# A decode step of attention and ReGLU on one core: the dummy products at the end taken out, and the first 26 rows of wo loaded and multiplied in two pieces

## The chip, the cores and the metric

The kernel runs on one core of a Trainium2 chip. The metric is the device time of one execution in microseconds. Beside it stands a profile of one execution: its span goes from the first to the last instruction, and its times are counted from the span's start.

## What is computed

Four sequences take one decode step. With x of shape (4, 1, 512):

```python
g = sigmoid((x * gate_w).sum(-1, keepdims=True))
q = (x @ wq) as 32 heads of 128
k, v = last 4096 rows of the caches of 8 heads, each shared by 4 heads of q
o = softmax(q k^T / sqrt(128)) v
a = o.reshape(4, 1, 4096) @ wo                 # wo: 4096 x 512
gate, up = x @ W_gate, x @ W_up                # 512 x 1792
b = (gate * (gate > 0) * up) @ W_down          # W_down: 1792 x 512
return g * a + (1 - g) * b
```

All inputs are bf16. K and V of the window are 32 MiB each, and the weights some 13 MiB together, so that the kernel reads 81 MB and computes little with it.

## The kernel before

**Staging.** Work on the caches goes in 8 sets (a sequence and half of its key heads), 4 MiB of K and 4 MiB of V each, in two buffers of each kind (`Ksb`, `Vsb`). All large loads are issued by SP in one order: wq, K and V by turns, W_gate and W_up into the buffer of K of set 6, the last V, W_down into the buffer of V of set 6, and then wo into `Wbig`, where wq was. SP waits with a load until PE has done with the buffer. The issue of W_down waits for the values of set 6, and the loads of wo stand behind it in SP's program.

**A set.** PE transposes K (line 366, f32 words that hold two bf16 each), ACT and DVE copy the result back (lines 371 and 373), PE forms the scores (line 387), DVE and ACT make the softmax's numerators (lines 395 to 431), PE multiplies them with V (line 442), and `combine` (lines 456 to 466) sums and scales into `oq`, already times g. PE's program for the sets from 2 on is a loop of three turns (`Fori`), and what follows the loop is written out.

**The end, which the change touches.** After the last set's scores PE runs, in this order: `combine` of set 6, `gateup` (line 472), the last set's `values` (line 442), its `combine`, and then the output products, which all sum into one bank of PSUM, `AB`:

- 56 products of `hT` with W_down (14 rows of 128-wide tiles, 4 column blocks `cb` each);
- the products of `oq` with wo. Each partition holds 32 rows of wo (`Wo3[:, i, :]`, i from 0 to 31), and each row gives 4 products of 128 columns, one for each column block.

Every product goes through `product` (line 543). The four column blocks sit in four 32-column strips of PE's array (`tile_position=(0, 32 * cb)`) and write to four strips of 32 partitions of the bank.

**The cuts of wo.** `WO_CUTS` names the rows at which the load of wo is cut: `(0, 26, 30)` makes a load of rows 0 to 25 (3328 KB, event `("WO", 0)`), one of rows 26 to 29 (512 KB, `("WO", 1)`), both at line 248, and then two of the last two rows, each of half the columns (128 KB each, `("WOL", u)`, line 251). The products of a piece wait for its load. The last 8 products end in two events `("ACC", u)`, for which DVE (line 568) and ACT (line 570) wait, each casting two blocks of 128 columns into `outr`. SP waits for the four casts and stores `outr` (line 594).

**The dummies.** `warm(n)` (line 548) issues n products of a 128x128 identity with 256 columns of `mask` into the bank `SCB[1]`, which nobody reads. Four stand ahead of each piece of wo that is cut by `WO_CUTS`, and four ahead of the last two rows: 12 in all.

**Waits.** `emit_list` gives an instruction a wait only where the engine hasn't already waited for that semaphore's value; every load of wo has a semaphore of its own.

Of the kernel before, what the change touches and what calls it, by code (L numbers as in the profile page):

```python
# [19 lines left out]
NSET = 8  # L20
# [8 lines left out]
NPIECE = 2  # L29
NBANK = 4  # L30
NFILL = 16
WO_CUTS = (0, 26, 30)
ACT_TAKES = (0, 1, 4, 6, 8, 9, 11, 13, 14)
LOOP_FIRST = 2
LOOP_TURNS = 3
# [107 lines left out]
def bass_gated_mix__sliding_block_cached__glu_gated_reglu__decode_kernel(  # L143
# [13 lines left out]
    with ExitStack() as ctx:  # L157
        def sb(name, shape, dt):
            return ctx.enter_context(nc.sbuf_tensor(name, shape, dt))
# [7 lines left out]
        mask = sb("mask", [128, 512], BF16)  # L167
        ident = sb("ident", [128, 128], BF16)
# [33 lines left out]
        SCB = banks[NTR:NTR + NSC]  # L202
# [10 lines left out]
        P = Program()  # L213
# [31 lines left out]
        wo_src = A_wo.rearrange("(p i) w -> p (i w)", p=128)  # L245
        for k in range(len(WO_CUTS) - 1):
            lo, hi = 512 * WO_CUTS[k], 512 * WO_CUTS[k + 1]
            P.dma("sp", lambda e, lo=lo, hi=hi: e.dma_start(Wbig[:, lo:hi], wo_src[:, lo:hi]), ("WO", k), [("Q",)])
        wo_src3 = A_wo.rearrange("(p i) w -> p i w", p=128)
        for u in range(2):  # L250
            P.dma("sp", lambda e, u=u: e.dma_start(Wo3[:, WO_CUTS[-1]:32, 256 * u:256 * u + 256],
                                                   wo_src3[:, WO_CUTS[-1]:32, 256 * u:256 * u + 256]), ("WOL", u), [("Q",)])

# [50 lines left out]
        for t in range(4):  # L304
            P.op("pe", lambda e, t=t: e.matmul(FB[:, 32:36], gwB[:, t * 128:(t + 1) * 128], xT[:, t, 0:4],
                                               start=(t == 0), stop=(t == 3)),
# [5 lines left out]
        for half in range(2):  # L312
            for t in range(4):
                for g in range(4):
# [3 lines left out]
                        start=(t == 0), stop=(t == 3), tile_position=(0, 32 * g)),  # L318
# [223 lines left out]
        def product(stat, mov, cb, start, stop, name, waits):  # L542
            P.op("pe", lambda e: e.matmul(AB[32 * cb:32 * cb + 4, 0:128], stat, mov[:, 128 * cb:128 * cb + 128],  # L543
                                          start=start, stop=stop, tile_position=(0, 32 * cb)), name, waits)

        def warm(n):
            for k in range(n):
                P.op("pe", lambda e: e.matmul(SCB[1][:, 0:256], ident[:, :], mask[:, 0:256], start=True, stop=True),  # L548
                     None, [("MASK",), ("SCC", NSET - 1, NBANK - 1), ("SCC", NSET - 1, 1)])

        for i in range(NFT):
            for cb in range(4):
                product(hT[:, 4 * i:4 * i + 4], Wd[:, i, :], cb, i == 0, False, None,
                        [("WD",), ("H",), ("SCC", NSET - 1, NBANK - 1)])
        for k in range(len(WO_CUTS) - 1):
            warm(4)
            for i in range(WO_CUTS[k], WO_CUTS[k + 1]):
                for cb in range(4):
                    product(oq3[:, :, i], Wo3[:, i, :], cb, False, False, None, [("WO", k), ("OQ", NSET - 1)])
        warm(4)  # L560
        for u in range(2):
            for i in range(WO_CUTS[-1], 32):
                for cb in (2 * u, 2 * u + 1):
# [76 lines left out]
```

## Time and profile before

| what | before |
|---|---|
| median of 3 runs | 199.1 us (198.62 to 200.11) |
| the profiled execution's own time | 199.63 us |
| its span | 198.4 us |
| mean granted TensorE clock | 0.871 |
| busy: PE, DVE, ACT, POOL | 138.5, 105.3, 63.8, 7.3 us |
| read from HBM | 81.01 MB, 408 GB/s over the span |

How to read it: the page cuts the span into 40 slices of 4.96 us and gives a digit for each, the busy share in tenths. PEclk is the share of TensorE's clock that was granted, 1.00 being full. In a list in order of time, a row has start, duration, engine, line, operation, the tile written and those read, and the shape; the bracket at the end is the idle time ahead of it and what ended that. PE's matmuls are pipelined: a group of n products that lasts t has not n times the mean duration of one, since they overlap, and the end of the group is the end of the last. The chain of waits is followed back from the last instruction, at each step to what released it.

### The profile page before, as it was taken

Reading aid. Unit: us, or ns where it says so; the run is one execution under the profiler, and the core shown is the slowest. Engines: PE = TensorE matmul, PEld = TensorE weight load, DVE = VectorE, ACT = ScalarE, POOL = GpSimd, SP = SyncE. Lnnn points to the kernel's source line nnn. Section 1 sums busy time; section 2 is a strip of 40 time slices with the busy share of each in tenths; the row PEclk is TensorE's granted clock in tenths of the full one; section 3 lists DMA queues with packets and bytes.
Section 4 is the critical chain, followed back from the end, with each engine's and each line's share of the span. In section 5 each row is a group of like instructions: output and inputs, shape, how many; then the busy total and the mean of one; then the engine's idle time right before and its main releaser. Section 6 shows DMA issues by size and latency. Waiting matters only on the chain.

```text
span 198.4 us, 3970 instructions
## 1 busy us (share of the span) xinstructions
PE 138.5 (70%) x1708; PEld 105.3 (53%) x1708; DVE 105.3 (53%) x282; ACT 63.8 (32%) x112; POOL 7.3 (4%) x37
## 2 busy tenths in 40 slices
PE   0135399689399939973997499759946996708446
PEld 0112387556288638743874487458626864206343
DVE  1204046895568557952785278529760986740101
ACT  2002135663074307511651165127503650400001
POOL 7300000000000000000000000000000000000000
PEclk9999999999759988995799669979995899666957
DMA  6999999999999999999999999999999999999950
GB/s 225 456 449 436 436 423 426 423 423 415 436 443 453 423 426 424 429 439 429 423 423 423 436 456 424 429 423 429 443 436 429 409 406 461 423 419 458 398 199 4
DMA packets 3741, 81.17 MB, mean 409 GB/s; under 512 B 393, under 2 KB 914, under 8 KB 1042
## 3 DMA queue, kind: packets, MB, share of 16 engines
q1 hardware_dynamic: 3720, 81.01, 95.6%
q8 instruction: 8, 0.13, 0.3%
q14 instruction: 3, 0.02, 0.0%
q10 hardware_dynamic: 10, 0.01, 0.0%
HBM read 81.01 MB, written 0.00 MB: 408 GB/s over the span
## 4 chain that ended last, share of the span: by engine, by line
DMA 58%; PE 34%; DVE 5%; issue 1%; SPq 0%; ACT 0%; DVEq 0%
DMA Ksb<-in_A_k_cache_dram 46%; PE bank L366 21%; DMA Wbig<-in_A_wo_dram 12%; PE bank L387 5%; DVE Ksb L373 3%; PE bank L442 2%; PE bank L543 2%; PE bank L456 2%; PE bank L548 1%; DVE sc L395 1%; DVE pT L431 1%; DVE mq L402 0%; ACT Ksb L371 0%; DVE negmax L416 0%; SPq L588 0%
## 5 line engine op out<-in xcount | busy, mean ns | idle before, releaser
L366 PE MATMUL bank<-identw,Ksb 128*128 128x128 f32 x512 | 79.4, 318 | 26.5 <-DMA Ksb<-in_A_k_cache_dram 26.5
L366 PEld LDWEIGHTS bank<-identw,Ksb 128*128 128x128 f32 x512 | 70.0, 166 | 36.1 <-DMA Ksb<-in_A_k_cache_dram 28.3
L371 ACT COPY Ksb<-bank 128x512 f32<-128x512 f32 x72 | 41.2, 586 | 87.6 <-PE bank L366 87.5
L373 DVE COPY Ksb<-bank 128x512 f32<-128x512 f32 x56 | 37.6, 685 | 43.7 <-PE bank L366 43.5
L395 DVE CUSTOM_DVE_ANT_0 sc<-bank,mask 128x512 bf16<-128x512 f32 x32 | 21.8, 680 | 7.5 <-PE bank L387 7.3
L442 PE MATMUL bank<-Vsb,pT 128*32 128x256 bf16 x512 | 20.7, 291 | 6.7 <-DMA Vsb<-in_A_v_cache_dram 6.7
L387 PE MATMUL bank<-Ksb,qS 128*32 128x512 bf16 x256 | 20.2, 391 | 4.3 <-DVE Ksb L373 4.1
L442 PEld LDWEIGHTS bank<-Vsb,pT 128*32 128x32 bf16 x512 | 13.4, 101 | 13.5 <-issue 9.8
L431 DVE STREAM_TRANSPOSE pT<-sc 128x1024 bf16<-128x1024 bf16 x16 | 19.7, 1236 | 1.4 <-ACT sc L424 1.3
L424 ACT ACTIVATE sc<-sc,negmax 128x1024 bf16<-128x1024 bf16 x16 | 18.4, 1150 | 5.3 <-DVE negmax L416 5.2
L456 PEld LDWEIGHTS bank<-osb,Wsel 128*64 128x64 f32 x128 | 8.2, 139 | 5.5 <-issue 2.9
L456 PE MATMUL bank<-osb,Wsel 128*64 128x32 f32 x128 | 9.1, 225 | 2.0 <-DVE osb L448 2.0
L387 PEld LDWEIGHTS bank<-Ksb,qS 128*32 128x32 bf16 x256 | 4.2, 95 | 11.5 <-DVE Ksb L373 6.5
L570 ACT CAST outr<-bank 4x128 bf16<-4x128 f32 x2 | 0.5, 258 | 25.0 <-PE bank L543 25.0
L543 PE MATMUL bank<-Wbig,oq 128*4 128x128 bf16 x128 | 3.8, 303 | 5.1 <-DMA Wbig<-in_A_wo_dram 5.1
L448 DVE COPY osb<-bank 128x256 f32<-128x256 f32 x8 | 3.4, 420 | 6.7 <-PE bank L442 6.7
L568 DVE CAST outr<-bank 4x128 bf16<-4x128 f32 x2 | 0.6, 282 | 11.6 <-PE bank L543 11.6
L298 PE MATMUL bank<-identw,xw 5*128 5x5 f32 x4 | 0.6, 264 | 8.5 <-DVE xw L292 8.5
L543 PEld LDWEIGHTS bank<-Wbig,oq 128*4 128x4 bf16 x128 | 3.1, 120 | 6.0 <-DMA Wbig<-in_A_wo_dram 5.4
L348 POOL COPY qS<-qW 128x64 bf16<-128x64 bf16 x8 | 1.8, 236 | 119.1 <-PE bank L387 106.6
L316 PE MATMUL bank<-Wbig,xT 128*32 128x512 bf16 x32 | 3.6, 631 | 3.0 <-DMA Wbig<-in_A_wq_dram 3.0
L416 DVE TENSOR_SCALAR negmax<-mall 32x1 f32<-32x1 f32 x32 | 4.6, 144 | 1.0
(60 smaller groups left out, 55.2 us busy)
## 6 DMA issues: line engine op xcount, KB each, us to landing
Ksb<-in_A_k_cache_dram SPq DMA_DIRECT2D x8, 4096.0 KB, 23.1
Vsb<-in_A_v_cache_dram SPq DMA_DIRECT2D x8, 4096.0 KB, 32.2
Wbig<-in_A_wq_dram SPq DMA_DIRECT2D x1, 4096.0 KB, 12.4
Wbig<-in_A_wo_dram SPq DMA_DIRECT2D x1, 3328.0 KB, 24.3
Ksb<-in_B_W_gate_dram SPq DMA_DIRECT2D x1, 1792.0 KB, 18.8
Ksb<-in_B_W_up_dram SPq DMA_DIRECT2D x1, 1792.0 KB, 22.7
Vsb<-in_B_W_down_dram SPq DMA_DIRECT2D x1, 1792.0 KB, 16.7
Wbig<-in_A_wo_dram SPq DMA_DIRECT2D x1, 512.0 KB, 25.1
```

Source lines behind the costliest of these rows:

```text
L316: P.op("pe", lambda e, half=half, t=t, g=g, col=col: e.matmul(SCB[half][32 * g:32 * g + 32, 0:512], xT[:, t, :], Wq3[:, t, col:col + 512], ...
L366: P.op("pe", lambda e, bk=bk, cc=cc, c=c, s=s: e.transpose(bk[:, cc * 128:(cc + 1) * 128], Kw[:, s % 2, c * 128:(c + 1) * 128], identw[:, :]),
L371: P.op("act", lambda e: e.copy(dst, bk[:, :]), ("KTC", s, i), [("KT", s, i)], sem="va")
L373: P.op("dve", lambda e: e.tensor_copy(dst, bk[:, :]), ("KTC", s, i), [("KT", s, i)], sem="vd")
L387: P.op("pe", lambda e, a=a, o=o: e.matmul(bk[32 * a:32 * a + 32, 0:512], qS[:, s % 2, o, :], k4[:, 16 * bank:16 * bank + 16, 32 * a:32 * a ...
L395: P.op("dve", lambda e: e.tensor_tensor_reduce(sc[:, s % 2, bank * 512:(bank + 1) * 512], bk[:, :], mask[:, :], 1.0, LOWEST, ALU.add, ALU.max,
L416: P.op("dve", lambda e, a=a: e.tensor_scalar(negmax[32 * a:32 * a + 32, par:par + 1], mall[:, 0:1], -SCALE, None, op0=ALU.mult), ("NEGMAX" ...
L424: P.op("act", lambda e: e.activation(sc[:, par, k * PW:(k + 1) * PW], sc[:, par, k * PW:(k + 1) * PW], ACTF.Exp, bias=negmax[:, par:par + ...
L431: P.op("dve", lambda e: e.transpose(pT[:, par, k * PW:(k + 1) * PW], sc[:, par, k * PW:(k + 1) * PW]), ("PTT", s, k), [("EXP", s, k), ("PV ...
L442: P.op("pe", lambda e, c=c, g=g, blk=blk: e.matmul(OB[32 * g:32 * g + 32, 0:256], pT[:, par, 32 * blk:32 * blk + 32], Vsb[:, par, 256 * bl ...
L456: P.op("pe", lambda e, k=k, lo=lo: e.matmul(FB[r, 384:416], Wsel[:, lo:lo + 64], osb[:, par, 32 * k:32 * k + 32], start=(k == 0), stop=(k ...
L543: P.op("pe", lambda e: e.matmul(AB[32 * cb:32 * cb + 4, 0:128], stat, mov[:, 128 * cb:128 * cb + 128], start=start, stop=stop, tile_positi ...
```

## The change

`WO_CUTS` gets one more cut, so that rows 0 to 25 come as a load of rows 0 to 15 (2048 KB) and one of rows 16 to 25 (1280 KB), each with a semaphore and a wait of its own; the products of rows 0 to 15 wait for the first alone. The order of the products is the same. `warm` and its three places are taken out. wo now comes in five loads.

```diff
-WO_CUTS = (0, 26, 30)
+WO_CUTS = (0, 16, 26, 30)
...
-        def warm(n):
-            for k in range(n):
-                P.op("pe", lambda e: e.matmul(SCB[1][:, 0:256], ident[:, :], mask[:, 0:256], start=True, stop=True),
-                     None, [("MASK",), ("SCC", NSET - 1, NBANK - 1), ("SCC", NSET - 1, 1)])
-
         for i in range(NFT):
             for cb in range(4):
                 product(hT[:, 4 * i:4 * i + 4], Wd[:, i, :], cb, i == 0, False, None,
                         [("WD",), ("H",), ("SCC", NSET - 1, NBANK - 1)])
         for k in range(len(WO_CUTS) - 1):
-            warm(4)
             for i in range(WO_CUTS[k], WO_CUTS[k + 1]):
                 for cb in range(4):
                     product(oq3[:, :, i], Wo3[:, i, :], cb, False, False, None, [("WO", k), ("OQ", NSET - 1)])
-        warm(4)
         for u in range(2):
             for i in range(WO_CUTS[-1], 32):
```

## The prediction

> **What bounds the kernel now.** I read the page's head and chain first, then the time order of the last 14 us, then the granted clock there, then the loads of wo.
>
> ```profile
> span 198.4 us, 3970 instructions
> DMA  6999999999999999999999999999999999999950
> DMA packets 3741, 81.17 MB, mean 409 GB/s; under 512 B 393, under 2 KB 914, under 8 KB 1042
> DMA 58%; PE 34%; DVE 5%; issue 1%; SPq 0%; ACT 0%; DVEq 0%
> ```
>
> The DMA engines are busy in every one of 40 slices but the first and the last two. Up to about 191 us the loads set the time and no edit in PE's program can be worth anything there. After the loads end, 7 us remain, and that is where this change lies. The order of work there (start, duration, engine, line):
>
> ```profile
> 185.06 0.28 PE L543 MATMUL bank<-Vsb,hT 128*4 128x128 bf16 x7
> 185.27 0.61 PE L548 MATMUL bank<-mask,ident 128*128 128x256 bf16 x4
> 191.01 2.95 PE L543 MATMUL bank<-Wbig,oq 128*4 128x128 bf16 x104 [5.13 <-DMA Wbig<-in_A_wo_dram]
> 193.89 1.03 PE L548 MATMUL bank<-mask,ident 128*128 128x256 bf16 x4
> 194.86 0.60 PE L543 MATMUL bank<-Wbig,oq 128*4 128x128 bf16 x16
> 195.39 0.80 PE L548 MATMUL bank<-mask,ident 128*128 128x256 bf16 x4
> 196.12 0.29 PE L543 MATMUL bank<-Wbig,oq 128*4 128x128 bf16 x8
> 196.44 0.54 ACT L570 CAST outr<-bank 4x128 bf16<-4x128 f32 x2 [24.97 <-PE bank L543]
> 196.44 0.60 DVE L568 CAST outr<-bank 4x128 bf16<-4x128 f32 x2 [11.57 <-PE bank L543]
> 197.06 0.35 SPq L594 DMA_DIRECT2D out_dram<-outr  x1
> ```
>
> PE has everything but wo done at 185.88, waits 5.1 us for the 26-row load, and then runs 104 products, four dummies, 16 products, four dummies, 8 products, end to end. The chain of waits says the same:
>
> ```profile
> 166.68 24.29 DMA Wbig<-in_A_wo_dram
> 190.97 0.04 issue
> 191.01 2.95 PE bank L543 x59
> 193.96 0.97 PE bank L548 x4
> 194.93 0.53 PE bank L543 x16
> 195.46 0.73 PE bank L548 x4
> 196.19 0.23 PE bank L543 x8
> 196.42 0.02 issue
> 196.44 0.28 DVE outr L568
> 196.72 0.32 DVEq L589
> ```
>
> So the tail is one load's landing at 190.97, then 5.45 us of PE, then 1.97 us of casts and the store. When did the other pieces of wo land? The SP queue's issues, with the time from issue to landing:
>
> ```profile
> 166.68 0.91 SPq L248 DMA_DIRECT2D Wbig<-in_A_wo_dram  x2
> 167.63 0.95 SPq L251 DMA_DIRECT2D Wbig<-in_A_wo_dram  x2
> Wbig<-in_A_wo_dram SPq DMA_DIRECT2D x1, 3328.0 KB, 24.3
> Wbig<-in_A_wo_dram SPq DMA_DIRECT2D x1, 512.0 KB, 25.1
> DMA to landing us min/median/max: 24.8/24.9/24.9
> ```
>
> (The last line is that of the two loads of line 251.) The second issue of each pair starts at 167.16 and 168.11, the end of the pair less one issue (0.43 and 0.47 us). Landings are then 190.97 (26 rows), about 192.25 (4 rows), 192.45 and 192.95 (the two half-width pieces of the last two rows). Everything is in memory at 192.95 and PE finishes 3.5 us later.
>
> **The dummies, which are removed: 12 products.** The first four (185.27) lie in the wait for wo and cost nothing. The other eight are on the path. The chain charges them 0.97 and 0.73 us, and between the starts of the products around them lie 194.86 - 193.89 = 0.97 and 196.12 - 195.39 = 0.73. Together 1.7 us. What did they buy? The granted clock (fourth figure from the end of a row, after POOL, is PEclk):
>
> ```profile
> 185.60:189.00 3.40, 0.28 (x3) 0.00 (x0) 0.00 (x0) 0.00 (x0) 0.00 (x0) 1.00 0.90 380
> 189.00:192.40 3.40, 1.39 (x56) 1.39 (x60) 0.00 (x0) 0.00 (x0) 0.00 (x0) 0.50 0.64 232
> 192.40:195.80 3.40, 3.40 (x83) 2.31 (x72) 0.00 (x0) 0.00 (x0) 0.00 (x0) 0.50 0.02 5
> 195.80:198.40 2.60, 0.61 (x11) 0.21 (x9) 0.56 (x2) 0.52 (x2) 0.00 (x0) 1.00 0.01 2
> ```
>
> The first four did not hold the clock over the wait: it is 0.50 from 189.0 to 195.8, and full only for the last eight products. Without dummies those eight run at 0.50: a product then lasts at most 315 ns instead of 219 (minimum and maximum of the row below), so 0.1 us is lost once.
>
> ```profile
> L543 PE MATMUL bank<-Wbig,oq x128: 219/311/315, 191.0 to 196.2; 128*4 128x128 bf16 x128
> ```
>
> The Trainium skill, "TensorE: Matmul & The Clock Gate", section "Why this matters for your kernels", speaks against this edit: it wants no PE idle gap over some 3 us between bursts, because the clock halves. The trace agrees that the clock halves after such a gap, but it did so with the dummies in place, so by the rule too this removal takes nothing away here.
>
> **The split of the 26-row load: 16 rows, then 10.** The same bytes in the same order, one DMA more on SP. SP issues at 0.43 us apiece, so the issues behind it move from 167.6 and 168.1 to about 168.1 and 168.5, 24 us ahead of their landing; SP's next instruction after them is the store, at 197. The cover is the loads queued ahead (W_down and the last V among them), and it would have to shrink by over 20 us before the issue showed. Cost nothing.
>
> The 16-row piece holds all but 10 x 512 x 2 bytes x 128 partitions = 1.31 MB of the old load, which at the mean 409 GB/s take 3.2 us. It lands at about 190.97 - 3.2 = 187.8, well behind PE's readiness at 185.3. From the row of 104 products the pace is (2.95 - 0.31) / 103 = 26 ns from start to start, with 0.31 us for the last to end. So its 64 products take 64 x 0.026 + 0.31 = 2.0 us: 187.8 to 189.8, wholly inside the wait for the 10 rows, with 1.2 us to spare. The 40 products of the 10 rows start at 191.0 and last 40 x 0.026 + 0.31 = 1.35 us, to 192.35, issue ending at 192.05. The 16 of the next piece now meet a wait that was hidden before: the load lands at 192.25, so they run 192.3 to 192.9 (0.60 us, the row at 194.86). The next piece landed at 192.45, so its four products follow until 193.0, and ACT and DVE make their first casts by 193.3 (0.28 us). The last four wait for the landing at 192.95, start at 193.0 and end at 193.3 (0.31 us). **The stall thus goes from PE to the last landing**: the load of the last two rows is late next, and nothing behind 192.95 can be shortened by faster products.
>
> What the fifth load costs itself is not in the trace of before. Lower bound zero. As a near row, the 512 KB load lands 1.28 us behind the one ahead of it, which is 410 GB/s, the mean rate of the kernel: no fixed cost between queued loads is seen. Upper bound: the output's 4 KB, a load by itself, take from 197.06 to the end of the span at 198.39, 1.33 us. I take 0.05, close to the queued row, which it is most like, and keep 1.3 for the range. The Trainium skill, "DMA: Bandwidth & Descriptors", section "Anatomy of one DMA — SWDGE (gpsimd) path", fits 2.0 us plus bytes over 436 GB/s for each DMA of the GpSimd path. If that held here and stood in the chain, the sum would gain only 1.4 us; the trace does not show it between loads that are queued.
>
> **The sum.** The second pair of casts, back to back with the first before, ended at 196.44 + 0.60 = 197.04. Now it starts at 193.3 + 0.05 (fifth load) and ends 0.28 later, at 193.65. The store follows as it did, 1.35 us to the end. Gain 197.04 - 193.65 = 3.4 us; the span goes from 198.4 to 195.0. Of that 1.7 are the dummies and 1.7 the 64 products moved under the load; by PE's count alone the split gives 64 x 0.026 = 1.66, so both ways agree, and the landing at 192.95 would cap any further gain.
>
> The profiled execution took 199.63 us, 1.24 more than its span; less 3.4 is 196.2. It is 0.5 over the median of the runs, 199.1, which less 3.4 is 195.7. Which of the two fits depends on why the runs spread from 198.62 to 200.11: if it is the loads, the new kernel shares it; if it is the clock in the last 7 us, the new kernel, which no longer waits for PE there, does not. I take the middle, **196.0 us**, 1.6% under the median.
>
> **Rivals.**
>
> *The products are not brought forward* (the 16-row piece lands late, or PE lacks something at 187.8, such as its own code, of which a block comes in over the same DMA engines at that time).
>
> ```profile
> q8 instruction: 2, 0.03, 1.3%
> ```
>
> Those are two blocks of 16 KB between 188 and 198 us, so PE does read code in the tail. Against it: 1.2 us of slack. If all of it failed, 128 products would follow 191.01 without a break, 128 x 0.026 + 0.31 = 3.6, ending at 194.6 instead of 196.42: the dummies' gain alone, 1.8 us, 197.8 by the profiled execution and 197.3 by the median: 197.5.
>
> *The last landing moves out* by the price of a load by itself, 1.33 us: 197.3. (With the Trainium skill's 2.0 us, from the page named above, it would be 198.0.) For it speaks that the end now hangs on that landing alone; against it the 1.28 us row.
>
> *Slower: the cut of wo into 16 KB out of every 32 KB.* Each partition's share of wo is 32 KB in a row; K's and V's loads read such shares whole, the old piece 26 KB of each, the new ones 16 and 10 KB. If memory served only half as fast when half of each share is asked for, the 3.41 MB (8.3 us at 409 GB/s) would take twice that, and the time would be 196.0 + 8.3 = 204.3. It decides from the point at which the loss exceeds 3.4 us: 11.7 us, under 290 GB/s. Against it: the 4-row load reads 4 KB of each 32 KB and came at 410 GB/s.
>
> *The change does less than it says*, because in other executions the clock is full in the tail and the dummies cost less.
>
> ```profile
> L548 PE MATMUL bank<-mask,ident x12: 273/338/422, 185.3 to 195.9; 128*128 128x256 bf16 x12
> L543 PE MATMUL bank<-Vsb,hT 128*4 128x128 bf16 x56 | 1.2, 219 | 0.1
> ```
>
> The four dummies at full clock follow each other at (0.61 - 0.27) / 3 = 0.11 us, those at half clock at (1.03 - 0.42) / 3 = 0.2, and the 56 products at full clock come at (1.2 - 0.22) / 55 = 18 ns apiece, not 26. Eight dummies would then be some 0.7 us cheaper and the 128 products 1.0 us. But that makes the kernel before shorter, not the new one longer: its end is the landing plus 0.3. It moves the ratio, not the 196.
>
> **How the numbers follow.** Forecast 0.67 (195.0 to 196.8: the loads' own spread of 1.5 us between the runs, and the two ways to place the sum). Products not brought forward, 0.14, at 197.5. Last landing later, 0.11, at 197.3. Slower by the cut, 0.04; the remaining 0.04 is a drift of the load rate, which at 1.7% over 81 MB would eat the gain. The range that leaves out two in ten is 195.0 to 197.6. A measurement of this kernel can tell about 1% from no change, so faster means under 197.1: all of the forecast but a little, and some four in ten of the two middle rivals, 0.77; within 1% 0.17; slower 0.06.
>
> **What would show it.** In the profile after, line 548's rows are gone; 64 products of line 543 start near 187.8 and end before 190; 40 start near 191.0; the groups of 16, 4 and 4 each stand behind an idle time that ends with wo's landing, the last near 193.0; casts end near 193.65; span 195.0. PEclk stays 0.50 in the last 5 us without harm. Wrong would be: products of the 16 rows that start after 189; a last landing after 193.5; the gap of products and casts not closing; or a gain that shows before 185 us, where nothing was changed.

## The result and the profile after

The changed kernel takes 196.34 us (median of 4 runs, 196.08 to 196.54) against 199.41 us for the kernel before (4 runs, one more than above, 198.62 to 200.11). The ratio is 0.9846, with a 95% interval from 0.9804 to 0.9888: 1.5% faster, some 3.1 us. The profiled execution took 196.08 us with a span of 194.8 us, against 199.63 and 198.4.

From the page of the changed kernel, the span, the DMA engines' slices, the packets and the chain's shares:

```profile
span 194.8 us, 3947 instructions
DMA  6999999999999999999999999999999999999993
DMA packets 3885, 81.17 MB, mean 417 GB/s; under 512 B 409, under 2 KB 930, under 8 KB 1058
DMA 60%; PE 32%; DVE 6%; issue 1%; ACT 1%; SPq 1%; DVEq 0%
```

The same bytes come in 144 packets more: 16 of them are under 512 B, and the other 128, one for each partition's share that is cut, are of 8 KB or more. All slices but the first and the last are now full, so the idle end has shrunk.

The last stretch in order of time, with the weight loads (PEld), since they carry the waits:

```profile
187.69 1.22 PEld L543 LDWEIGHTS bank<-Wbig,oq 128*4 128x4 bf16 x64 [2.79 <-DMA Wbig<-in_A_wo_dram]
187.69 1.51 PE L543 MATMUL bank<-Wbig,oq 128*4 128x128 bf16 x64 [2.61 <-DMA Wbig<-in_A_wo_dram]
190.80 0.95 PEld L543 LDWEIGHTS bank<-Wbig,oq 128*4 128x4 bf16 x40 [1.89 <-DMA Wbig<-in_A_wo_dram]
190.80 2.34 PE L543 MATMUL bank<-Wbig,oq 128*4 128x128 bf16 x64 [1.60 <-DMA Wbig<-in_A_wo_dram]
192.05 0.52 PEld L543 LDWEIGHTS bank<-Wbig,oq 128*4 128x4 bf16 x20 [0.30 <-DMA Wbig<-in_A_wo_dram]
192.75 0.10 PEld L543 LDWEIGHTS bank<-Wbig,oq 128*4 128x4 bf16 x4 [0.18 <-DMA Wbig<-in_A_wo_dram]
192.90 0.54 ACT L563 CAST outr<-bank 4x128 bf16<-4x128 f32 x2 [21.84 <-PE bank L543]
192.90 0.59 DVE L561 CAST outr<-bank 4x128 bf16<-4x128 f32 x2 [8.58 <-PE bank L543]
193.53 0.35 SPq L587 DMA_DIRECT2D out_dram<-outr  x1
```

PE now waits for wo four times: 2.6 us for the 16 rows, 1.6 us for the 10, and in the weight loads 0.30 us for the 4 rows and 0.18 us for the last half piece. Before, it waited once and then had everything. The products end at 190.80 + 2.34 = 193.14, where they ended at 196.41. The chain of waits (its middle):

```profile
166.75 24.00 DMA Wbig<-in_A_wo_dram
190.75 0.04 issue
190.80 1.24 PE bank L543 x30
192.04 0.01 issue
192.05 0.83 PE bank L543 x20
```

It goes back to the landing of the 10 rows at 190.75, and names none of the later ones. The records of products overlap, so the two short waits behind 190.80 leave no gap in PE's row; only the weight loads show them. The last load lands at 168.2 + 24.5 = 192.7, 0.05 us ahead of the last four products.

### The profile page after: what moved, and what is told of

Same layout as the page of the kernel before. It is cut to its first block, busy times and chain, and to the rows that moved or that the text cites. A ratio compares the mean times of both kernels' runs of the same rounds, so it can differ in the third digit from the quotient of the medians.

```text
span 194.8 us, 3947 instructions
## 1 busy us (share of the span) xinstructions
PE 135.3 (69%) x1696; PEld 103.3 (53%) x1696; DVE 105.2 (54%) x282; ACT 63.8 (33%) x112; POOL 7.3 (4%) x37
## 4 chain that ended last, share of the span: by engine, by line
DMA 60%; PE 32%; DVE 6%; issue 1%; ACT 1%; SPq 1%; DVEq 0%
DMA Ksb<-in_A_k_cache_dram 47%; PE bank L366 21%; DMA Wbig<-in_A_wo_dram 12%; PE bank L387 5%; DVE Ksb L373 3%; PE bank L442 2%; PE bank L456 2%; PE bank L543 1%; DVE sc L395 1%; DVE pT L431 1%; ACT Ksb L371 1%; DVE mq L402 0%; DVE negmax L416 0%; SPq L248 0%; SPq L581 0%
## 6 DMA issues: line engine op xcount, KB each, us to landing
Wbig<-in_A_wo_dram SPq DMA_DIRECT2D x1, 2048.0 KB, 21.4
Ksb<-in_B_W_up_dram SPq DMA_DIRECT2D x1, 1792.0 KB, 21.4
Vsb<-in_B_W_down_dram SPq DMA_DIRECT2D x1, 1792.0 KB, 16.9
```

## Experiments

Five of the seven kernels take the change apart or test the clock and the price of a load; two move the cut. In each the kernel before ran on the same chip: 199.72 us (14 runs, 198.78 to 200.25) beside the first four, 199.12 us (7 runs, 198.78 to 199.88) beside the last three.

**The split alone**

```diff
-WO_CUTS = (0, 26, 30)
+WO_CUTS = (0, 16, 26, 30)
...
-            warm(4)
+            if WO_CUTS[k] != 16:
+                warm(4)
```

> The split alone: rows 0 to 25 in pieces of 16 and 10 rows, and the twelve dummies kept where they were (ahead of row 0, of row 26 and of the last two rows). Theory (the end is the later of PE's chain and the last landing): 64 products move under the load of the 10 rows, 64 x 0.026 = 1.7 us, and the eight dummies stay on PE's path with 1.7 us; products end near 194.7 in the profile, 1.7 us before the old 196.4, span 196.7, ratio 0.991. Rival that the dummies alone made the gain: products of rows 0 to 15 start no earlier than 190 or their head start is lost again, span 198.4, ratio 1.00. Rival that the split alone made it: span 195.0, ratio 0.983.

Measured: 198.18 us (7 runs, 197.34 to 198.54), ratio 0.9929 (0.9902 to 0.9955). Its PE in order of time:

```profile
187.94 1.07 PE L543 MATMUL bank<-Wbig,oq 128*4 128x128 bf16 x64 [0.33 <-DMA Wbig<-in_A_wo_dram]
191.06 1.05 PE L543 MATMUL bank<-Wbig,oq 128*4 128x128 bf16 x40 [2.05 <-DMA Wbig<-in_A_wo_dram]
192.05 1.03 PE L548 MATMUL bank<-mask,ident 128*128 128x256 bf16 x4
193.01 0.60 PE L543 MATMUL bank<-Wbig,oq 128*4 128x128 bf16 x16
193.54 1.03 PE L548 MATMUL bank<-mask,ident 128*128 128x256 bf16 x4
194.51 0.37 PE L543 MATMUL bank<-Wbig,oq 128*4 128x128 bf16 x8
```

The 64 products run at 187.94 as in the full change, and the two groups of dummies still hold the rest up by 193.01 - 192.05 = 0.96 and 194.51 - 193.54 = 0.97 us. Products end at 194.88, near the expected 194.7. Both rivals fall, since 1.00 and 0.983 lie outside the interval: the split gives a part of the gain, and not all of it.

**The dummies taken out alone**

```diff
-WO_CUTS = (0, 16, 26, 30)
+WO_CUTS = (0, 26, 30)
```

(against the changed kernel)

> The dummies taken out alone, the load of 26 rows left whole. Theory: 128 products follow the landing at 191.0 without a break, 128 x 0.026 + 0.31 = 3.6 us, to 194.6; span 196.6, ratio 0.991, and the two halves of the change add up to the whole. Rival that the split alone made the gain (the dummies' time was hidden or paid for by a fuller clock): span 198.4, ratio 1.00. Rival that the dummies alone made it: 195.0, ratio 0.983.

Measured: 197.70 us (6 runs, 197.63 to 197.99), ratio 0.9912 (0.9886 to 0.9938).

```profile
191.18 3.58 PE L543 MATMUL bank<-Wbig,oq 128*4 128x128 bf16 x128 [5.79 <-DMA Wbig<-in_A_wo_dram]
```

128 products in one stretch, 3.58 us where 3.6 was expected, to 194.76; span 196.7 us. Both rivals, 1.00 and 0.983, lie outside the interval. The two halves lose 0.71% and 0.88%, together 1.59%, and the whole change lost 1.54%: within the intervals they add up.

**The clock held up over the wait, in the kernel before**

```diff
-            warm(4)
+            warm(44 if k == 0 else 4)
```

> The kernel before with 44 dummies instead of four ahead of row 0, so that PE is busy for nearly all of its 5.1 us wait for wo; the other eight dummies stay. If the granted clock in the tail is what such products can buy: PEclk is 1.00 from 185 to the end, the 128 products come at some 19 ns instead of 26 (0.9 us less), the eight dummies on the path cost 0.7 us less, products end near 194.8, ratio 0.992, and the runs of it lie closer together than those of the kernel before. If the clock does not follow such products: PEclk 0.50 in the tail, products end near 196.4, ratio 1.00.

Measured: 197.92 us (8 runs), ratio 0.992 (0.9891 to 0.9949). The runs do not lie closer together: four at 197.31 to 197.39, with a mean granted clock of 0.89 to 0.90, and four at 198.44 to 198.87, at 0.85 to 0.86. The profiled one is of the second kind, and its products end at 195.13 + 0.29 = 195.42, where 194.8 was expected:

```profile
186.50 5.72 PE L548 MATMUL bank<-mask,ident 128*128 128x256 bf16 x44
192.15 1.63 PE L543 MATMUL bank<-Wbig,oq 128*4 128x128 bf16 x104
193.71 0.61 PE L548 MATMUL bank<-mask,ident 128*128 128x256 bf16 x4
194.25 0.40 PE L543 MATMUL bank<-Wbig,oq 128*4 128x128 bf16 x16
```

And its clock, by the column PEclk (third from the end):

```profile
185.60:189.00 3.40, 3.40 (x53) 2.64 (x45) 0.12 (x1) 0.00 (x0) 0.00 (x0) 0.64 0.88 376
189.00:192.40 3.40, 3.40 (x50) 2.88 (x51) 0.00 (x0) 0.00 (x0) 0.00 (x0) 1.00 0.68 243
192.40:195.00 2.60, 2.60 (x124) 2.03 (x112) 0.00 (x0) 0.00 (x0) 0.00 (x0) 1.00 0.02 6
```

The dummies do buy the full clock, and at full clock the 104 products take 1.63 us instead of 2.95. But the first dummies ran at half clock themselves, so that 44 of them took 5.72 us and started row 0 at 192.15, some 1.2 us behind the landing of its load (issued at 166.40, it took 24.5 us). In the faster four runs the dummies presumably ran at the full clock from the start and ended in time; no profile was taken of one, so this is an inference from the mean clock and the 1.1 us between the groups. What is shown: at full clock the 104 products, on which the end hangs here, take 1.3 us less.

**Dummies in PE's waits only, in the changed kernel**

```diff
+            warm((20, 6, 0)[k])
             for i in range(WO_CUTS[k], WO_CUTS[k + 1]):
```

(against the changed kernel; the definition of `warm` comes back with it)

> The changed kernel with dummies only inside PE's two waits for wo: 20 ahead of row 0 and 6 ahead of row 16, none behind. Theory: the end hangs on the last landing, so that the clock in the tail, full or half, moves it by at most 0.1 us: ratio to the kernel before as that of the changed kernel, 0.985, products end 0.3 to 0.45 us after the last landing. Rival that the clock still sets the end: PEclk 1.00 in the tail and span down by 0.4 us or more against the changed kernel's 194.8, ratio 0.982 or less.

Measured: 196.22 us (6 runs, 196.12 to 196.46), ratio 0.9839 (0.9813 to 0.9865), the changed kernel's 0.9846 again. Its PE, its chain and its clock:

```profile
189.61 1.07 PE L543 MATMUL bank<-Wbig,oq 128*4 128x128 bf16 x64
191.37 0.73 PE L543 MATMUL bank<-Wbig,oq 128*4 128x128 bf16 x40
192.38 0.98 PE L543 MATMUL bank<-Wbig,oq 128*4 128x128 bf16 x24 [0.28 <-DMA Wbig<-in_A_wo_dram]
...
168.36 24.68 DMA Wbig<-in_A_wo_dram
193.04 0.04 issue
193.08 0.30 PE bank L543 x4
...
189.00:192.40 3.40, 3.12 (x121) 2.32 (x120) 0.00 (x0) 0.00 (x0) 0.00 (x0) 1.00 0.71 254
192.40:195.00 2.60, 0.89 (x24) 0.39 (x24) 0.56 (x2) 0.52 (x2) 0.00 (x0) 0.97 0.04 9
```

The clock is full from 189 on (0.97 over the last stretch), the 64 and the 40 products start 1.9 and 0.6 us later than in the changed kernel, because dummies stand ahead of them, and neither matters: the chain's last load lands at 193.04 and the products end 0.34 us behind it (0.43 in the changed kernel, at half clock). The end follows the landing, and the clock is worth 0.1 us. The rival falls by the span: 195.0 us, and not 194.4 or less.

**The cut at row 4, and at row 24**

```diff
-WO_CUTS = (0, 16, 26, 30)
+WO_CUTS = (0, 4, 26, 30)      # the other: (0, 24, 26, 30)
```

> The changed kernel with the first cut at row 4 instead of 16: pieces of 4, 22, 4 and the last rows. Theory: only 16 products run ahead; 88 start at the landing near 190.75 and with the 24 behind them PE is the bound again: 112 x 0.0265 + 0.31 = 3.3 us, to 194.1, 0.95 us later than the changed kernel's 193.1; span 195.8; the groups behind do not wait for their loads. Rival that any split gives the whole gain (the end is the landing alone): products end at 193.1, span 194.8.

> The changed kernel with the first cut at row 24: pieces of 24, 2, 4 and the last rows. Theory: the first piece lands 2 x 128 KB = 0.6 us ahead of the 190.75 of rows 0 to 25, at 190.15; then 128 products without a break, 128 x 0.0265 + 0.31 = 3.7 us, to 193.85, 0.7 us later than the changed kernel; span 195.5. Rival that any split gives the whole gain: products end at 193.1, span 194.8.

Measured: 197.51 us (ratio 0.9911, 0.9881 to 0.994) and 197.35 us (0.9903, 0.9874 to 0.9933), four runs each. Cut at 4, then cut at 24:

```profile
185.29 0.40 PE L543 MATMUL bank<-Wbig,oq 128*4 128x128 bf16 x16
191.08 3.16 PE L543 MATMUL bank<-Wbig,oq 128*4 128x128 bf16 x112 [5.39 <-DMA Wbig<-in_A_wo_dram]
...
190.63 3.58 PE L543 MATMUL bank<-Wbig,oq 128*4 128x128 bf16 x128 [5.47 <-DMA Wbig<-in_A_wo_dram]
```

In both PE runs its remaining products without a break, so it is the bound again: they end at 194.24 and 194.21, 1.1 us later than in the changed kernel. Expected were 0.95 and 0.7. The start of 191.08 is 0.28 us later than the changed kernel's 190.80, since the loads of that execution landed later (W_down, ahead of them, at 183.0 instead of 182.8); the rest, 0.8 us, is the missing overlap. With the cut at 24 the first landing came at 190.59, not at 190.15, and W_down's at 183.15. Both spans are 196.2 us, more than the expected 195.8 and 195.5, also because all casts now start behind the last product (194.28 and 194.25), where the changed kernel's first start at 192.90, ahead of it. So not any split gives the gain, but one where the products behind each landing are issued before the next load lands. At 26 ns apiece, the cut at 4 leaves 88 products, 2.3 us, behind a landing that the next follows after 1.2 us; the cut at 24 leaves 96, 2.5 us, behind one that the next follows after 0.6.

**Ten loads for the first 30 rows**

```diff
-WO_CUTS = (0, 16, 26, 30)
+WO_CUTS = (0, 4, 8, 12, 16, 19, 22, 24, 26, 28, 30)
```

> The changed kernel with wo's first 30 rows in ten loads instead of three (cuts at 4, 8, 12, 16, 19, 22, 24, 26 and 28), seven loads more. Theory (0.05 us for a load that is queued): from the landing of W_down to the last landing of wo 9.95 us in the changed kernel, here 10.0 to 10.4; span 194.8 to 195.2. By a price of 1.33 us for each load, that of a load by itself, the last landing would come 9 us later and the time would be near 205. One price in between would show as its seventh part.

Measured: 196.81 us (4 runs, 196.59 to 197.81), ratio 0.9893 (0.9854 to 0.9932), span 195.3 us where 194.8 to 195.2 was expected. The issues and the times to landing, first of the changed kernel, then of this one (W_down, then the loads of line 251):

```profile
165.91 0.33 SPq L243 DMA_DIRECT2D Vsb<-in_B_W_down_dram  x1
167.70 0.95 SPq L251 DMA_DIRECT2D Wbig<-in_A_wo_dram  x2
Vsb<-in_B_W_down_dram SPq DMA_DIRECT2D x1, 1792.0 KB, 16.9
DMA to landing us min/median/max: 24.5/24.6/24.7
...
165.95 0.33 SPq L243 DMA_DIRECT2D Vsb<-in_B_W_down_dram  x1
166.32 14.98 SPq L248 DMA_DIRECT2D Wbig<-in_A_wo_dram  x10
181.35 3.40 SPq L251 DMA_DIRECT2D Wbig<-in_A_wo_dram  x2
Vsb<-in_B_W_down_dram SPq DMA_DIRECT2D x1, 1792.0 KB, 16.9
DMA to landing us min/median/max: 10.8/11.2/11.6
```

W_down lands at 165.91 + 16.9 = 182.8 and at 165.95 + 16.9 = 182.85. The last load is issued at 168.2 and lands 24.5 us later, at 192.7; here it is issued at 182.4 and lands 10.8 us later, at 193.25. From the one to the other landing are 9.9 and 10.4 us, where 10.0 to 10.4 was expected: seven more loads cost 0.4 to 0.5 us, 0.06 to 0.07 each, as far as one execution of each kernel tells. The price of 1.33 us is out.

## Why the prediction was right

**The path.** It held at each step: the loads set the time, and PE's long stall turned into short waits, the last for the last landing, as forecast. The table sets the prediction's times beside the profile's:

| step | predicted | measured |
|---|---|---|
| 64 products start | 187.8 | 187.69 |
| 40 products start | 191.0 | 190.80 |
| the 16 meet a wait | 192.3 | 192.05 |
| last four start | 193.0 | 192.75 |
| casts end | 193.65 | 193.49 |
| span | 195.0 | 194.8 |

From the second row on, the measured times are 0.15 to 0.25 us early. W_down, ahead of the change in the queue, landed at 166.31 + 16.7 = 183.0 before and at 182.8 here, so that this is the load queue of one execution and not a gain of the change. One sign was drawn wrongly: of the groups of 16, 4 and 4 only the first and the last stand behind a wait. The other 4 follow the 16 at once, as the prediction's own sum had it.

**The dummies.** 1.7 us was predicted; taken out alone they gave 0.88% of 199.72 us, 1.76 us. The first four of them did not hold the clock, as read from PEclk. (That is the third figure from the end of a window's row, and not the fourth, as the prediction says; the values that it takes, 0.50 and 1.00, are PEclk's.)

**The split.** 1.7 us was predicted, 0.71% or 1.4 us was measured for it alone, with an interval (0.9 to 2.0 us) that holds 1.7. In the profile of `split_only` both groups of dummies on the path ran at half clock and cost 0.96 and 0.97 us, where the second had cost 0.73 in the profile before; that would account for most of the difference. The sum over both held: 3.4 us forecast, 3.1 us measured.

**The fifth load.** 0.05 us was taken from the row of a queued load, and 0.06 to 0.07 came out as the mean of seven more. The fifth alone can't be read: from W_down's landing to the last lie 9.95 us with four loads and 9.9 with five. The upper bound of 1.33 us, and with it the rival that the last landing moves out, had no ground; its row was not a load but the store of the output, with the end of the program in it. The Trainium skill ("DMA: Bandwidth & Descriptors", section "Anatomy of one DMA — SWDGE (gpsimd) path") gives 2.0 us for each DMA of the GpSimd path. It is not seen between loads that SP has queued: seven of them cost 0.5 us, not 14.

**The cut of wo** into a part of every 32 KB: no loss. The loads of 4 KB pieces in `many` kept the pace: the products of two of them, 512 KB each, started as these landed, at 186.71 and 188.00, which is 406 GB/s.

**Code blocks.** For the rival that the products are not brought forward, the prediction took two blocks on the instruction queue as PE's code. The row names no engine, so that is not shown. The 64 products, at 187.69, did not wait for more than their load, which landed at 166.28 + 21.4 = 187.68.

**Off in size, off the path:** the 64 products took 1.51 us, not 2.0. They met the end of a stretch at full clock, as the changed kernel's windows show:

```profile
185.60:189.00 3.40, 1.31 (x64) 1.22 (x64) 0.00 (x0) 0.00 (x0) 0.00 (x0) 0.88 0.98 407
189.00:192.40 3.40, 1.79 (x64) 1.27 (x56) 0.00 (x0) 0.00 (x0) 0.00 (x0) 0.50 0.70 255
192.40:194.80 2.40, 0.74 (x20) 0.26 (x8) 0.56 (x2) 0.52 (x2) 0.00 (x0) 0.50 0.03 9
```

**Where the sum was placed.** The prediction took the middle between 196.2, by the profiled execution, and 195.7, by the median, and left open whether the runs before spread because of the loads or the clock. The median of 196.34 sides with 196.2. The range was laid out by a spread of the loads of 1.5 us, and the spans of the runs say otherwise. In the six kernels without dummies on the path they lie within 0.2 to 0.3 us of each other (194.8 to 195.1 in the changed kernel, 196.4 to 196.7 in `nodummy_only`), and in the three with them (`split_only`, `before_wait44`, the kernel before) within 1.1 to 1.5. (One run of `many` took 197.81 us, but its span of 195.5 lies among the others.) The same bytes are loaded in all, so the spread goes with the dummies on the path, and the new kernel sheds it. That would have been a reason to take 196.2. How they spread the runs stays open. It is not just that products on the path hang on the clock: `nodummy_only`, `cut4` and `cut24` end on PE's products too. And the mean granted clock tells the two groups of `before_wait44` apart, but in the kernel before a run of 198.78 us had 0.835 and one of 199.68 us had 0.88.

## What to carry to other kernels

Where loads end last, compare PE's readiness with each landing: work that stands between two landings is free as long as it takes less time than the next load, and a cut in a load is worth just the products that it moves there. Place the cut so that the products behind each landing are issued before the next; here cuts at rows 4 and 24 each ended the products 1.1 us later than the cut at row 16. Products that only keep the clock up belong into waits, and they have to end before the wait does; on the path, eight of them cost 1.7 us here, and the full clock that they ended with was worth 0.1.

## What was not expected of the hardware

SP's issues do not stay at 0.43 us when many loads are queued. In `many` the longest of line 248 took 5.73 us, others 1.0 to 2.7 us, and the last load was issued 11 us later than at the changed kernel's pace (twelve issues 0.47 us apart from 166.32 on would have it at 171.5):

```profile
L248 SPq DMA_DIRECT2D Wbig<-in_A_wo_dram x10: 432/432/5729, 166.3 to 180.3; - x10
```

The last load was issued at 182.4 and still landed in order, so here it was hidden; a store or a load for another buffer that SP issues behind such a queue would, by these rows, have waited.

The second: at full clock four products of 128 columns, in four strips of the array, come nearly twice as fast as at half clock. 104 of them took 1.63 us in `before_wait44`, (1.63 - 0.22) / 103 = 14 ns apiece against 26, where 18 ns was estimated from the products of W_down. That row held an idle 0.30 us of the weight loads; in `nodummy_only` the same 56 products took 0.95 us, 13 ns apiece. The Trainium skill ("TensorE: Matmul & The Clock Gate", section "Why this matters for your kernels") asks for no idle gap over some 3 us; the runs agree on the clock (1.00 in the tail with the wait filled, 0.50 without), but in the changed kernel a full clock moved the end by 0.1 us, since the end is a landing.
